# A recurrence and two expert layers: the router's ranks move behind U's products, one list is loaded earlier

## The chip, the cores and the metric

The kernel runs on one core of a Trainium2 chip. The metric is the device time of one execution in microseconds (us), from its first to its last instruction and what lies around them. Engines: PE (TensorE, matmuls), DVE (VectorE), ACT (ScalarE), POOL (GpSimd) and SP (SyncE, which issues DMAs here).

## The reference

Three stages follow one another: a recurrence over 768 steps (4 batches, 8 heads, dimension 40), a mixture of 8 experts with one expert chosen per token, and a second such layer with a bias by modality.

```python
for t in range(S):
    y[:, :, t] = np.einsum('bhd,bhde->bhe', rt, state)
    Sa = np.einsum('bhde,bhe->bhd', state, at)
    state_decay = state * wt[:, :, None, :] - np.einsum('bhd,bhe->bhde', Sa, bt)
    state = state_decay + np.einsum('bhd,bhe->bhde', vt, kt)
...
logits = x @ w_gate
expert_idx = np.argmax(logits, axis=1)
...
for e in range(E):
    mask = expert_idx == e
    ...
    h = np.maximum(xe @ w1[e], 0.0)
    ye = h @ w2[e]
    out[mask] = gate_w[mask, None] * ye
```

Tokens are the 3072 pairs of batch and step, with 320 features each (8 heads of 40); N = 3072, D = 320, E = 8, F = 1024.

## The kernel before

**Attention (some 45 to 500 us).** The 768 steps are cut into 24 chunks of 32 (`cc`, written c0 to c23 here). The instructions stand in the order in which the code issues them (`tc.manual_schedule()`, loop L743 to L849), and each engine works through its own queue in that order. A chunk issues on PE, one after the other: `x_v` (tile `xps`, L524), the transposes of the token rows of chunk cc−2 (`hook1`, `xt`, L1669), `x_z` (`xps`, L526 or L531), the transposed state (`sps`, L572), y's products of the chunk before (`yps`, L610), U's products (`ups`, L542, which ACT copies into `vu`, L546), the first half of y (`yps`, L600), z's products (`zz`, L557, added into the state `zs` by DVE, L563 and L565), `vps` (L582) and `cps` (L591, masked into `csb` by DVE, L594). Between these stand matmuls that prepare chunks ahead: `aps`, `kps`, `aab` (L336, L349, L361; DVE masks `aab` into `ak`, L366). A table `plan` says in which chunks this A-work is done: 13 of the chunks from c3 on (c3, c4, c6, c7, c8 to c16).

On DVE a list of filler work (`fl`, L397 and L403 and others: a triangular solve, transposes and decays of later chunks) is spread between the steps by `fl.run`. Each call issues a share of it; so the order on DVE is fixed when the kernel is built. The same holds for `PADS`, a table of matmuls of no use (`wps`, L883) that keep PE occupied; an entry hangs on a step by name. Two entries hang on `rp`: eleven in c3 and two in c8.

**The router inside the attention.** For the tokens of a finished chunk the loop does the first layer's routing in four steps, spread over three chunks:

- y's product is multiplied by the gate into the token rows `x` (DVE L1662) and stored (POOL's queue, L1663);
- `hook1` (chunk cc−2): transposes `xt`;
- `hook2` (chunk cc−2): the logits `lp` (PE L1677), and `choose` on DVE (`mx`, `dl`, `tb`, `fi`, `oh`, `ent`: L973 to L981) with the exponential on ACT (L975). In the 13 chunks of `plan` it stands right behind U's products, in the others behind `v_t`;
- `hook3` (chunk cc−3): three small matmuls `rp` (PE L990, L991, L992), which count the tokens of each expert up to each token from `oh`, the running counts `ccnt` (POOL L993) and the experts' bases; `tq`, `ps`, `posi` on DVE (L999, L1000, L1002) pick each token's rank; an indirect DMA on POOL's queue (L1011) scatters the token's entry to its place in the list `lst[0]`.

`lp`, `rp` and `aab` use the same PSUM tag "ac" with one buffer (`bufs=1`), so each waits until the one before it has been read.

**Experts (from some 500 us).** Rows are worked in blocks. For a block, `load1` and `load2` bring its weights (SP's queue, L1210 to L1216), `entries` brings its part of the list (`le`, SP's queue, L1250), `gather` fetches the token rows by it (`xg`, POOL's queue, L1257), and `put` stores rows (L1369). In `block(b, prev, nxt)` the work for the block after is issued inside the work for `b`: `entries(nxt)` (unless `begun`), `load1(nxt)`, `gather(nxt)`, and at the end `load2(nxt)`. The first call is `block(b0, a0, b1, begun=True)`; in the next one, `block(b1, b0, bs[1])`, the list of `bs[1]` is loaded.

Of the kernel before, what the change touches and what calls it, by code (L numbers as in the profile page):

```python
# [55 lines left out]
def attention(tc, zones, ident, r, k, v, w, a, b, emit_x, hook0, hook1, hook2, hook3, unsafe, extra, tail):  # L56
    nc = tc.nc
    with ExitStack() as ctx:
        cp = ctx.enter_context(tc.tile_pool(name="a_const", bufs=1))
        wp = ctx.enter_context(tc.tile_pool(name="a_work", bufs=2))  # L60
        ps = Warm(tc, ctx.enter_context(tc.tile_pool(name="a_psum", bufs=1, space=PSUM)), ident)
# [8 lines left out]
        cut = lambda z, at, *shape: view(zones[z], at, *shape)  # L70
# [17 lines left out]
        def guard_load(i):  # L88
            nc.sync.dma_start(out=gtile[i], in_=w.rearrange("b h (z s) d -> (b h z) (s d)", z=4)[:, GN * i : GN * i + GN])
# [73 lines left out]
        def load_a(st, cs=range(4)):  # L163
            st["ar"] = ar = cut("pa", (L + 1) * D, 4, H, D)
            for c in cs:
                t0 = (4 * st["g"] + c) * L
                for bb in range(4):
                    nc.sync.dma_start(out=ar[32 * bb : 32 * bb + 32, c], in_=a[bb, :, t0 : t0 + L, :].rearrange("h t d -> t h d"))
# [489 lines left out]
        def solve_ops(st):  # L658
            ops = solve(st)
            return [(0.19 if 0 < i < len(ops) - 1 else 1.2, f) for i, f in enumerate(ops)]  # L660

        with tc.manual_schedule():
# [80 lines left out]
            for cc in range(NCH):  # L743
                g, c = cc // 4, cc % 4
                nx = Chunk(sts[(cc + 1) // 4], (cc + 1) % 4, rv[cc + 1]) if cc + 1 < NCH else None
                slots = late
                late = [[] for _ in range(8)]
                for ca, how in plan.get(cc, []):
                    sa, ga = sts[ca // 4], ca // 4
                    fs = chunk_a(sa, ca % 4)  # L750
                    if ca % 4 == 3 and ga + 1 < NG:
                        slots[LOADA].append(lambda ga=ga: load_a(sts[ga + 1]))
                    for sl, f in zip(HOW[how], fs):
                        if sl < 0:
                            f()
                        elif sl < 10:
                            slots[sl].append(f)
                        else:
                            late[sl - 10].append(f)
                    if ca % 4 == 3:  # L760
                        def start(sa=sa, ga=ga):
                            if ga == 1:
                                so = hv2.ops()
                                so[0]()
                                fl.add(cc, 2, [(0.14 if i < 60 else 1.8, f) for i, f in enumerate(so[1:])])
                                fl.add(3, 4, [(0.2, f) for f in hv2.rest()])
                            else:
                                so = solve_ops(sa)
                                so[0][1]()
                                fl.add(cc, 4 * ga - 1, so[1:])  # L770
                        (late[{2: 1, 5: 0, 7: 1}[how]] if how in (2, 5, 7) else slots[6]).append(start)

                if cc == 0:
                    nc.gpsimd.memset(kbt[2], 0.0)
                    hv2 = Halves(sts[1])
                if cc == 1:
                    late[0].append(hv2.begin)
                if cc == GUARD:
                    guard_load(0)
                    guard_load(1)  # L780
                    gd = guard_ops(0)
                    gd.append(lambda f=gd.pop(): (f(), guard_load(2)))
                    gd += guard_ops(1) + guard_ops(2)

                def slot(i):
                    if GUARD < cc < VERDICT and i in (1, 2, 4, 5) and gd:
                        gd.pop(0)()
                    for f in todo.get((cc, i), []) + slots[i]:
                        f()
                    for f in extra.get((cc, i), []):  # L790
                        f(ps)
                    if (cc, i) in halves:
                        halves[cc, i]()

                fl.begin(cc)
                ps.at(cc)
                cur.x_v()
                if cc > 2:
                    hook3(cc - 3, ps)
                if cc > 1:  # L800
                    hook1(cc - 2, ps, ident)
                slot(0)
                if cc == 2:
                    hook0(1)
                if cc == VERDICT:
                    verdict()
                cur.x_z()
                cur.s_t(0)
                fl.run(0.2)
                slot(1)  # L810
                if prev:
                    prev.y_c()
                cur.s_t(1)
                fl.run(0.15)
                if nx:
                    nx.r_t()
                if cc + 2 < NCH:
                    rv.append(load_r(cc + 2))
                slot(7)
                cur.u_()  # L820
                fl.run(0.1)
                slot(2)
                if cc > 1 and plan.get(cc):
                    hook2(cc - 2, ps)
                fl.run(0.1)
                cur.y_s()
                fl.run(0.15)
                slot(3)
                fl.run(0.1)
                cur.z_()  # L830
                if cc == 0:
                    spread_ops(sts[1])[3]()
                if nx:
                    cur.z_up(nx.st["qlf"], nx.c)
                slot(4)
                cur.v_t()
                if cc + 2 < NCH:
                    load_v(cc + 2, rv[cc + 2])
                if cc == 0:
                    hook0(0)  # L840
                slot(5)
                if cc > 1 and not plan.get(cc):
                    hook2(cc - 2, ps)
                fl.run(0.07)
                cur.c_()
                slot(6)
                fl.run(0.13)
                fl.drain(cc)
                prev, cur = cur, nx  # L849
# [41 lines left out]
def view(t, at, *shape):  # L891

    n = int(np.prod(shape))
    names = [f"d{i}" for i in range(len(shape))]
    v = t[:, at : at + n]
    return v.rearrange(f"p ({' '.join(names)}) -> p {' '.join(names)}", **dict(zip(names[1:], shape[1:]))) if len(shape) > 1 else v
# [261 lines left out]
class Block:  # L1158
    def __init__(self, lay, tab, j, cut=None, first=False, ready=False, own=None):

        self.lay, self.tab, self.j, self.first, self.ready, self.own = lay, tab, j, first, ready, own
        self.cut, self.i = cut or lay.cut, None


class Rows:
# [23 lines left out]
class Experts:  # L1189
# [56 lines left out]
    def entries(self, b):  # L1246
        nc, c = self.nc, b.cut
        self.place(b)
        r = nc.values_load(b.tab["reg"][0:1, 2, b.j : b.j + 1], engines=[ET.SP], min_val=0, max_val=LST - c.tb)
        d = nc.sync.dma_start(out=b.le, in_=b.lay.lst[ds(r, c.tb)].rearrange("(h p) w -> p h w", p=c.g))  # L1250
        if self.loose and not b.lay.route:
            self.lrows.after(d.ins)
# [125 lines left out]
    def block(self, b, prev, nxt, hook=None, begun=False):  # L1378
# [12 lines left out]
                self.place(x)  # L1391
        if nxt is not None:
            if not begun:
                self.entries(nxt)
                self.load1(nxt)
                put(0, lambda: self.gather(nxt))
        for q in range(0 if b.ready else 4):
# [198 lines left out]
def network(tc, r, k, v, w, a, b, moe_w_gate, moe_w1, moe_w2, moe2_modality_id, moe2_w_gate, moe2_modality_bias, moe2_w1, moe2_w2, out):  # L1596
    nc = tc.nc
    with ExitStack() as ctx:
# [30 lines left out]
        ex = Experts(tc, wt, ident, rt)  # L1629
# [11 lines left out]
        with tc.tile_pool(name="n_x", bufs=1) as xp:  # L1641
# [38 lines left out]
            def hook3(cc, ps):  # L1680
                rps[cc] = rp = ps.tile([P, 1, NE], F32, tag="ac", name="rp", bufs=1)
                rt.rank(rp)
                rt.scatter(rt.rows(rp), ent[:, cc : cc + 1], lst[0])
# [59 lines left out]
        with ExitStack() as ctx2:  # L1743
# [44 lines left out]
            with tc.manual_schedule():  # L1788
                bs = [b1] + [Block(l1, b1.tab, j) for j in range(1, n1)]
                ex.loose = True  # L1790
                ex.load1(b1)
                ex.gather(b1)
                for h in range(CUT0.h):
                    ex.put(a0, h)
                ex.block(b0, a0, b1, begun=True)
                prev = b0
                for b_, nxt in zip(bs, bs[1:]):
                    ex.block(b_, prev, nxt)
                    prev = b_
                t2 = rt.ahead(tp, 1, CUT2, 2, counts(tp, 1))  # L1800
                more = [Block(l2, t2, j, first=j == 0) for j in range(2)]
                ex.block(bs[-1], prev, more[0])
                tabs = []
                ex.block(more[0], bs[-1], more[1], lambda: tabs.append(rt.table(tp, 2, CUT2, counts(tp, 2), t2)))
                ex.run(more[1:] + [Block(l2, tabs[0], j) for j in range(n2)])
# [18 lines left out]
```

## Time and profile before

| | us |
|---|---|
| median of 3 runs | 1011.77 |
| lowest and highest run | 1007.17, 1011.89 |
| profiled execution, its own time | 1014.81 |
| span in its trace (first to last instruction) | 1012.6 |
| PE busy in the span | 896.7 |
| DVE busy | 695.9 |
| ACT busy | 506.5 |
| POOL busy | 308.8 |

The mean granted TensorE clock of the profiled execution is 0.940 of full speed. The shares are means over two very different parts; what a wait in the attention is worth is read from the windows and timelines there. In a timeline a row is a run of like instructions: its start, its duration, the engine, the line, what it writes and reads, and in brackets how long the engine had been idle before it and what ended that.

### The profile page before, as it was taken

The page shows a single profiled execution, that of the slowest core. Times are in us where ns is not written, and L with a number is a line of the kernel's source. Part 1 is how long each engine was busy: PE and PEld are TensorE (multiplying, and loading weights), DVE is VectorE, ACT ScalarE, POOL GpSimd, SP SyncE. Part 2 cuts the span into 40 slices and gives each one's busy share as a digit, 9 for nine tenths or more (in the row PEclk, how much of TensorE's full clock was granted, in tenths as well). Part 3 has the DMA queues.
Part 4 walks back from the last instruction along what each step waited for, and adds up shares of the span by engine and source line. Part 5 has one row for each costly group of instructions (what it writes and reads, how often), then busy time and mean ns, then how long its engine had stood idle before and what let it go on. Part 6 is the DMA issues. An engine that isn't in the chain of part 4 may idle for free. (4 is left out here: it accounts for less than half of the span.)

```text
span 1012.6 us, 38223 instructions
## 1 busy us (share of the span) xinstructions
PE 896.7 (89%) x16089; PEld 828.0 (82%) x16089; DVE 695.9 (69%) x2023; ACT 506.5 (50%) x991; POOL 308.8 (30%) x361
## 2 busy tenths in 40 slices
PE   8748888887878898877979899999999999999995
PEld 8647777676767787766869899999999999999995
DVE  7799999998997966833545354554554866776762
ACT  6625445454535676624414244444544565665662
POOL 6550021221221210122133325453443433323321
PEclk9769989899989999978889899999999999999998
DMA  5545445443432642325017253535343111371110
GB/s 181 138 131 118 75 106 110 113 99 86 97 87 50 165 93 52 55 68 125 11 39 204 83 138 106 147 89 146 109 137 82 27 47 47 90 208 41 43 38 27
DMA packets 152421, 96.41 MB, mean 95 GB/s; under 512 B 127407, under 2 KB 139585, under 8 KB 151850
## 3 DMA queue, kind: packets, MB, share of 16 engines
q1 hardware_dynamic: 138154, 72.53, 28.6%
q0 software_dynamic: 14080, 21.28, 8.2%
q8 instruction: 130, 2.13, 0.9%
q14 instruction: 57, 0.47, 0.2%
HBM read 112.18 MB, written 14.59 MB: 125 GB/s over the span
## 5 line engine op out<-in xcount | busy, mean ns | idle before, releaser
L1301 PE MATMUL hp<-xs,h 128*128 128x256 f32 (+1 forms) x840 | 156.9, 317 | 0.0
L1312 PE MATMUL yp<-h,hh 128*114 128x320 f32 (+1 forms) x464 | 147.0, 317 | 0.3 <-DMA s<-moe_w 0.3
L1313 PE MATMUL yp<-l,hh 128*114 128x320 f32 (+1 forms) x464 | 144.4, 311 | 0.0
L1314 PE MATMUL yp<-h,hl 128*114 128x320 f32 (+1 forms) x464 | 144.2, 311 | 0.0
L1304 DVE SCALAR_TENSOR_TENSOR hl<-hp,hh 128x456 fp32r<-128x456 f32 (+1 forms) x116 | 76.6, 660 | 90.7 <-ACT hh L1303 90.7
L1301 PEld LDWEIGHTS hp<-xs,h 128*128 128x128 f32 x840 | 124.4, 190 | 3.3
L1303 ACT ACTIVATE hh<-hp 128x456 fp32r<-128x456 f32 (+1 forms) x116 | 66.5, 573 | 110.3 <-PE hp L1301 105.9
L1301 PE MATMUL hp<-xs,l 128*128 128x256 f32 (+1 forms) x504 | 102.5, 312 | 0.0
L1222 DVE TENSOR_TENSOR l<-s,h 128x768 fp32r<-128x768 f32 x88 | 80.7, 956 | 11.0 <-ACT h L1221 8.7
L1312 PEld LDWEIGHTS yp<-h,hh 128*114 128x114 f32 (+1 forms) x464 | 85.4, 184 | 0.6 <-ACT hh L1303 0.5
L1313 PEld LDWEIGHTS yp<-l,hh 128*114 128x114 f32 (+1 forms) x464 | 85.5, 184 | 0.2
L1314 PEld LDWEIGHTS yp<-h,hl 128*114 128x114 f32 (+1 forms) x464 | 85.2, 184 | 0.0
L1257 POOL DMA_INDIRECT xg<-x,le x52 | 61.5, 1182 | 70.7 <-issue 50.7
L1301 PEld LDWEIGHTS hp<-xs,l 128*128 128x128 f32 x504 | 80.1, 190 | 3.1
L1228 DVE TENSOR_TENSOR l<-s,h 128x640 fp32r<-128x640 f32 x88 | 72.6, 825 | 3.2 <-ACT h L1227 3.2
L1369 POOL DMA_INDIRECT out<-yo,ti x28 | 34.0, 1215 | 129.4 <-ACT yo L1365 74.7
L1221 ACT CAST h<-s 128x768 fp32r<-128x768 f32 x88 | 70.4, 835 | 0.2
L1227 ACT CAST h<-s 128x640 fp32r<-128x640 f32 x88 | 63.3, 719 | 0.0
L1011 POOL DMA_INDIRECT lst<-l2e,posi x32 | 40.4, 1263 | 59.7 <-DVE posi L1004 52.4
L993 POOL TENSOR_TENSOR ccnt<-ccnt,oh 128x8 bf16<-128x8 bf16 x24 | 6.4, 267 | 168.9 <-PE rp L991 145.7
L1275 DVE TENSOR_TENSOR xs<-ta,xs 128x456 fp32r<-128x456 f32 (+1 forms) x28 | 18.5, 662 | 55.6 <-ACT xs L1274 55.4
L1274 ACT CAST xs<-ta 128x456 fp32r<-128x456 f32 (+1 forms) x28 | 15.8, 564 | 79.3 <-PE ta L1271 79.3
(365 smaller groups left out, 2021.4 us busy)
## 6 DMA issues: line engine op xcount, KB each, us to landing
s<-moe_w SPq DMA_DIRECT2D x22, 1280.0 KB
s<-moe_w SPq DMA_DIRECT2D x22, 1024.0 KB
s<-moe_w SPq DMA_DIRECT2D x44, 256.0 KB
z_w<-w SPq DMA_DIRECT2D x40, 160.0 KB
z_kb<-k SPq DMA_DIRECT2D x24, 160.0 KB
z_kb<-b SPq DMA_DIRECT2D x24, 160.0 KB
z_pa<-a SPq DMA_DIRECT2D x96, 40.0 KB
rt<-r SPq DMA_DIRECT2D x96, 40.0 KB
```

The source lines that it names most:

```text
L1011: d = self.nc.gpsimd.indirect_dma_start(out=dst, out_offset=IndirectOffsetOnAxis(ap=pi[:, i : i + 1], axis=0), in_=ent[:, i], in_offset=No ...
L1221: nc.scalar.copy(wt["h1"][:, :, s], wt["s1"][:, :, s])
L1222: nc.vector.tensor_sub(wt["l1"][:, :, s], wt["s1"][:, :, s], wt["h1"][:, :, s].bitcast(F32))
L1227: nc.scalar.copy(wt["h2"][:, s], wt["s2"][:, s])
L1228: nc.vector.tensor_sub(wt["l2"][:, s], wt["s2"][:, s], wt["h2"][:, s].bitcast(F32))
L1257: d = self.nc.gpsimd.indirect_dma_start(out=b.xg[:, h], out_offset=None, in_=b.lay.src, in_offset=IndirectOffsetOnAxis(ap=b.le[:, h, 0:1]. ...
L1301: nc.tensor.matmul(out=hp[:, i], lhsT=l, rhs=r, start=k == 0, stop=k == len(ops) - 1)
L1303: nc.scalar.activation(hh[:, s], hp, AF.Relu)
L1304: nc.vector.scalar_tensor_tensor(out=hl[:, s], in0=hp, scalar=0.0, in1=hh[:, s].bitcast(F32), op0=ALU.max, op1=ALU.subtract)
L1312: nc.tensor.matmul(out=yp, lhsT=hh[:, k, t], rhs=wt["h2"][:, k], start=k == 0, stop=False)
L1313: nc.tensor.matmul(out=yp, lhsT=hh[:, k, t], rhs=wt["l2"][:, k], start=False, stop=False)
L1314: nc.tensor.matmul(out=yp, lhsT=hl[:, k, t], rhs=wt["h2"][:, k], start=False, stop=k == 7)
```

## The change

`hook3`, with everything that it issues (three matmuls on PE, three operations on DVE, one operation and one indirect DMA on POOL, and the pads that hang on `rp`), moves from behind `x_v` to behind U's products. In the 13 chunks of `plan` it then stands directly ahead of `hook2`. In the experts' part the list of `bs[1]` is loaded before the first `block` call, and a flag `listed` keeps `block` from loading it again.

```diff
                 cur.x_v()
-                if cc > 2:
-                    hook3(cc - 3, ps)
                 if cc > 1:
                     hook1(cc - 2, ps, ident)
...
                 cur.u_()
+                if cc > 2:
+                    hook3(cc - 3, ps)
                 fl.run(0.1)
                 slot(2)
                 if cc > 1 and plan.get(cc):
                     hook2(cc - 2, ps)
...
-        self.cut, self.i = cut or lay.cut, None
+        self.cut, self.i, self.listed = cut or lay.cut, None, False
...
     def entries(self, b):
         nc, c = self.nc, b.cut
         self.place(b)
+        b.listed = True
...
             if not begun:
-                self.entries(nxt)
+                if not nxt.listed:
+                    self.entries(nxt)
                 self.load1(nxt)
...
+                ex.entries(bs[1])
                 ex.block(b0, a0, b1, begun=True)
```

On PE, c9, around U's products (`ups`), before:

```order
L513 MATMUL rps<-ident,rt 80x128 x4
L349 MATMUL kps<-ident,z_wide 128x128 x4
L542 MATMUL ups<-xs,tt 32x40 x32
L1677 MATMUL lp<-wg_123,xT 128x128 x3
L883 MATMUL wps<-ident 128x128 x2
L600 MATMUL yps<-ssb,rb_158 32x40 x32
```

and after (lines behind L1660 are numbered two higher):

```order
L349 MATMUL kps<-ident,z_wide 128x128 x4
L542 MATMUL ups<-xs,tt 32x40 x32
L990 LDWEIGHTS tri
L990 MATMUL rp<-oh_119,tri 128x8
L991 LDWEIGHTS ones
L991 MATMUL rp<-ccnt,ones 128x8
L992 LDWEIGHTS ones
L992 MATMUL rp<-ebr,ones 128x8
L1679 MATMUL lp<-wg_123,xT 128x128 x3
L883 MATMUL wps<-ident 128x128 x2
L600 MATMUL yps<-ssb,rb_158 32x40 x32
```

The six instructions of `rp`, which stood behind `x_v` (L524) of the same chunk, now stand between `ups` and `lp`.

On DVE, c9, before (`pr` and `z_sol` are the solve's filler work, the transpose to `z_wide` too):

```order
L397 TENSOR_TENSOR pr<-z_sol 128x42
L999 TENSOR_TENSOR tq_120<-rp,oh_119 128x8
L1000 TENSOR_REDUCE ps_115<-tq_120 128x1
L1002 CAST posi_121<-ps_115 128x1
L239 STREAM_TRANSPOSE z_wide<-z_kb 128x40x2x16
L397 TENSOR_TENSOR pr<-z_sol 128x45
L403 TENSOR_TENSOR z_sol<-z_sol,pr 128x14x3
L403 TENSOR_TENSOR z_sol<-z_sol,pr 128x15x3
L397 TENSOR_TENSOR pr<-z_sol 128x56 x2
L403 TENSOR_TENSOR z_sol<-z_sol,pr 128x14x4 x2
L397 TENSOR_TENSOR pr<-z_sol 128x65
L1662 TENSOR_TENSOR x<-yps,gt_151 128x320
```

and after, the same stretch from the filler ahead of `x` on:

```order
L397 TENSOR_TENSOR pr<-z_sol 128x65
L1664 TENSOR_TENSOR x<-yps,gt_151 128x320
L397 TENSOR_TENSOR pr<-z_sol 128x70
L403 TENSOR_TENSOR z_sol<-z_sol,pr 128x13x5
L403 TENSOR_TENSOR z_sol<-z_sol,pr 128x14x5
L397 TENSOR_TENSOR pr<-z_sol 128x78 x2
L403 TENSOR_TENSOR z_sol<-z_sol,pr 128x13x6
L999 TENSOR_TENSOR tq_120<-rp,oh_119 128x8
L1000 TENSOR_REDUCE ps_115<-tq_120 128x1
L1002 CAST posi_121<-ps_115 128x1
L403 TENSOR_TENSOR z_sol<-z_sol,pr 128x13x6
L397 TENSOR_TENSOR pr<-z_sol 128x84
```

The three operations `tq`, `ps`, `posi`, which stood ahead of the transpose and of `x`, now stand behind `x`, between two filler operations of L403, a few rows ahead of `mx` (L973), the first reader of `lp`.

On SP's queue, in the experts' part (`s` is the weights' staging buffer: L1212 writes the last of `load1(b1)`, L1216 is `load2(b1)`; `le` is the list of `bs[1]`), before:

```order
L1212 DMA s_9270<-moe_w 64x1024
L1216 ISA
L1216 DMA s_9271<-moe_w 128x8x320
L1249 TENSOR_LOAD small
L1249 ISA x2
L1250 ISA
L1250 DMA le_14600<-lst_61 114x4x4
```

and after:

```order
L1212 DMA s_9270<-moe_w 64x1024
L1250 TENSOR_LOAD small
L1250 ISA x2
L1251 ISA
L1251 DMA le_14600<-lst_61 114x4x4
L1216 ISA
L1216 DMA s_9271<-moe_w 128x8x320
```

The load of the list now stands ahead of that of the weights' second part.

## Rows read from the trace of the kernel before

**Rows 1.** Windows: busy us by engine, early and late stretch.

```profile
core 0: us, PE busy (x) PEld busy (x) DVE busy (x) ACT busy (x) POOL busy (x), PEclk, DMA share, GB/s
150.00:200.00 50.00, 41.81 (x1389) 35.47 (x1388) 48.93 (x158) 24.45 (x56) 10.37 (x13) 0.93 0.50 112
...
450.00:500.00 50.00, 42.23 (x1278) 35.99 (x1276) 19.91 (x55) 23.20 (x52) 9.11 (x12) 0.84 0.34 87
```

**Rows 2.** PE by line, 100:500: busy, mean | idle before, until.

```profile
L990 PE MATMUL rp<-oh,tri 128*128 128x8 bf16 x22 | 3.9, 176 | 12.4 <-DVE oh L980 6.4 <-DVE z_ak L366 4.2 <-DVE ak L366 1.7
```

**Rows 3.** Waits of DVE, 100:500 us: total, times, longest.

```profile
DVE x L1662 <- PE yps L610: 18.8, 10, 4.3
DVE mx L973 <- PE lp L1677: 12.2, 8, 3.0
```

**Rows 4.** Timeline of DVE, c3: start, duration, operation [idle before].

```profile
138.75 0.49 DVE L1662 TENSOR_TENSOR x<-yps,z_gt 128x320 f32<-128x320 f32 x1 [0.55 <-PE yps L610]
```

**Rows 5.** Timeline of DVE, c11.

```profile
295.12 0.49 DVE L1662 TENSOR_TENSOR x<-yps,gt 128x320 f32<-128x320 f32 x1 [1.61 <-PE yps L610]
```

**Rows 6.** Timeline of PE, beginning of c3.

```profile
129.41 0.18 PE L990 MATMUL rp<-oh,tri 128*128 128x8 bf16 x1 [3.17 <-DVE oh L980]
...
129.65 0.61 PE L1669 MATMUL xt<-ident,x 128*128 128x128 f32 x3
```

**Rows 7.** Timeline of all engines, c13, where lp follows tq.

```profile
331.23 0.16 DVE L999 TENSOR_TENSOR tq<-rp,oh 128x8 f32<-128x8 f32 x1
...
331.45 0.38 PE L1677 MATMUL lp<-wg,xT 128*128 128x128 f32 x1 [0.34 <-DVE tq L999]
```

**Rows 8.** Timeline of PE, c9, from U's products to z's.

```profile
256.81 1.33 PE L542 MATMUL ups<-xs,tt 32*32 32x40 f32 x64
258.06 1.13 PE L1677 MATMUL lp<-wg,xT 128*128 128x128 f32 x6
...
260.97 0.80 PE L600 MATMUL yps<-ssb,rb 128*32 128x40 f32 x64 [1.13 <-DVE x L1662]
...
262.73 1.44 PE L557 MATMUL zz<-vu,kb 128*40 128x80 f32 x32
```

**Rows 9.** Timeline of DVE, c9.

```profile
261.54 1.58 DVE L403 TENSOR_TENSOR z_sol<-z_sol,pr 128x78 f32<-128x78 f32 x2
...
263.52 0.15 DVE L973 TENSOR_REDUCE mx<-lp 128x1 f32<-128x8 f32 x1
...
266.99 0.82 DVE L563 TENSOR_TENSOR zs<-zz,zs 128x640 f32<-128x640 f32 x1
```

**Rows 10.** Timeline of all engines, a late chunk's rp and tq.

```profile
451.41 0.18 PE L990 MATMUL rp<-oh,tri 128*128 128x8 bf16 x1
...
451.76 0.17 DVE L999 TENSOR_TENSOR tq<-rp,oh 128x8 f32<-128x8 f32 x1 [0.38 <-PE rp L992]
```

**Rows 11.** Timeline of SP's queue: weights' second part, then the list.

```profile
533.29 0.39 SPq L1216 DMA_DIRECT2D s<-moe_w  x1
534.84 0.33 SPq L1250 DMA_DIRECT2D le<-lst  x1
```

**Rows 12.** Timeline of ACT: first cast of those weights.

```profile
551.05 0.72 ACT L1227 CAST h<-s 128x640 fp32r<-128x640 f32 x1
```

**Rows 13.** Timeline of POOL: first gather of the block.

```profile
559.25 1.21 POOL L1257 DMA_INDIRECT xg<-x,le  x1 [8.12 <-issue]
```

**Rows 14.** Windows at the beginning of c6.

```profile
190.00:192.00 2.00, 0.14 (x2) 0.13 (x2) 1.79 (x9) 0.21 (x1) 1.67 (x2) 0.86 0.44 73
192.00:197.00 5.00, 5.00 (x142) 4.13 (x141) 4.93 (x12) 1.37 (x4) 0.50 (x2) 0.50 0.60 159
```

**Rows 15.** Timeline of PE at the lower clock: lp and z's products.

```profile
446.79 1.94 PE L1677 MATMUL lp<-wg,xT 128*128 128x128 f32 x6
...
463.63 2.37 PE L557 MATMUL zz<-vu,kb 128*40 128x80 f32 x32
```

**Rows 16.** Timeline of PE: the gathered rows are waited for.

```profile
571.93 0.45 PE L1271 MATMUL ta<-ident,xg 114*128 114x114 f32 x1 [3.85 <-DMA xg<-x,le]
```

## The prediction, made before the changed kernel was run

> **What bounds the kernel now.** I read the windows first. In a window of the early chunks DVE is busy 48.93 us of 50 and PE 41.81; in a window of the last chunks DVE is at 19.91 and PE at 42.23 of 50, at a granted clock of 0.84 [rows 1]. So the attention part has two regimes. Up to about chunk 13 (c13; c8 and c12 are partly exceptions) DVE is the bound, and a wait of PE costs nothing until DVE runs out of work. Later the chain from PE to ACT to DVE and back is the bound, and PE work on it counts in full. Then I read what the moved `rank` matmuls wait for: PE sits 12.4 us before their first matmul, until `oh` or `ak` come from DVE [rows 2]. That looks like a prize, but the view of waits on DVE decides: what DVE itself loses to y's products (`x`) is 18.8 us in 10 waits, and to the logits (`lp`) 12.2 us in 8 [rows 3]. Of the waits for `x`, only two stand in a DVE-bound chunk in which PE had waited before rp: 0.55 us in c3 [rows 4] and 1.61 us in c11 [rows 5].
>
> **What goes.** Between the start of rp and the first transpose behind it lie 129.65 − 129.41 = 0.24 us of PE [rows 6], and in front of rp there is the wait. Both leave the chunk's beginning. In c3 (wait 3.17 us) and c11 DVE gets back no more than its own gap, 0.55 and 1.61; I count 1.75 for c11, because its later products also gain the 0.24. In the late chunks c17 to c22 rp stands on PE's path at the beginning, and its new place behind U's products lies under ACT's copies of U, for which `zz` waits anyway: 6 x 0.24 = 1.44. In c23 a wait of 0.57 goes too: 0.81. Gains: 0.55 + 1.75 + 1.44 + 0.81 = 4.55 us.
>
> **What comes.** In the 13 chunks that still plan A-work, the logits' matmuls follow rp directly. rp and lp share one PSUM buffer (tag "ac"), so lp can't start before `tq` on DVE has read rp. In the kernel before this wait shows once, in c13: lp sits 0.34 us until tq, and starts 0.06 us behind tq's end [rows 7]. Behind lp, on PE's queue, stand y's, z's, v's and c's products; DVE waits for all of them. Two prices follow, by what DVE is doing.
>
> Where DVE is the bound, tq waits for its turn. In c9 its new turn is behind the first of the two L403 at 261.54, which end together at 263.12, the second taking some 0.15: so tq starts at about 262.95 and ends at 263.1, and lp starts at 263.2 instead of 258.06, 5.1 us later [rows 8, 9]. Behind it PE has the same products as before up to zz's end, which came at 262.73 + 1.44 = 264.17, that is 6.11 us behind lp's start, with a wait of 1.13 for `x` among them that is over by then. So zz ends at 263.2 + 4.98 = 268.2, where `zs` of the kernel before started at 266.99. DVE has the same work up to there in both kernels (three rank operations are merely moved), so DVE loses 1.2 us; of the 5.1 us, 3.9 are swallowed by slack. The same reading in c6, c11 and c13 (lp later by 3.5, 5.2 and 4.1 us, the slack of `mx`, `zs` and `csb` taken one by one) gives 0.8, 0.5 and 0.5. In c3, c4, c7 and c10 the slack covers all. Sum 3.0.
>
> Where DVE waits for PE (c8, c12, c14, c15, c16), tq follows rp at once. Where DVE stood ready in the kernel before, rp started at 451.41 and its tq at 451.76, 0.35 later, and lasted 0.17 [rows 10]; with the 0.06 of the way back lp is 0.58 us later, less the 0.24 that left the beginning: 5 x 0.34 = 1.7. Bounds: 5 x 0 if DVE's other waits take it all, 5 x 0.58 = 2.9 if the beginning gives nothing back.
>
> Edits at nothing. POOL's `ccnt` and the scatter now stand behind x's store; POOL is busy 10.37 of 50 us in the early window [rows 1], and the lists are first read after the attention. On DVE three small operations are moved, none added. The eleven and two warming matmuls that hang on rp in c3 and c8 go with it into time in which PE waits (c3) or some tenths (c8, inside the bound of 2.9). The second edit puts the load of `le` ahead of `load2(b1)` on SP's queue: from 533.29 and 534.84 [rows 11] to the reverse order, load2 about 1.5 us later. Its first reader is ACT's cast at 551.05 [rows 12], over 15 us later. The gather that reads `le` comes at 559.25 [rows 13] either way, since it follows the rows that the puts before it store. Zero.
>
> Without the clock: 3.0 + 1.7 − 4.55 = +0.15 us.
>
> **The clock.** The granted clock is the term that decides the sign. In c6 PE had 0.14 us of work in the two microseconds before rp, and from 192 to 197 the clock is 0.50, that is 1.2 GHz [rows 14]. Seven of the eight waits of 2.4 us or more between 129 and 464 us have such a stretch right behind them. The Trainium skill, "TensorE: Matmul & The Clock Gate", section "What's actually happening", says that "the default state is throttled, and activity releases the throttle"; the rows of c6 agree. The rule speaks against this change: by it alone all four new waits would be followed by the half clock, the time of the first rival below. The change makes four new waits of 3.5 to 5.2 us, in c6, c9, c11 and c13, and each lies directly ahead of matmuls whose slack is by then used up. At the half clock lp takes 1.94 instead of 1.13, zz 2.37 instead of 1.44 [rows 8, 15]: 0.81 + 0.93 = 1.74 us for each such chunk. c6 and c11 already have a half-clock stretch, which may only move. For c9 and c13 I take even odds: 2 x 1.74 / 2 = +1.74. Bounds: nothing, or 4 x 1.74 = 6.96.
>
> Sum: 0.15 + 1.74 = +1.9 us. On the profiled run (span 1012.6, its own time 1014.81) that is 1016.7; that run stands 3.04 us above the median of the runs, 1011.77, so I state the forecast against the median: **1013.7 us**. About 0.5% (5 us) is what a measurement of this kernel can tell from no change; the three runs of before differ by 4.7 us among themselves.
>
> **Rivals.**
> *The clock falls in all four chunks* (slower). Mechanism: PE stands behind lp's wait for tq, the clock drops to 1.2 GHz, and lp, zz and what follows come late for DVE, which has no slack left. It decides from two full stretches on. For it: c6's rows, and seven waits of eight. Against it: DVE had filler work in c6 that hid a half-clock stretch completely. Price 0.15 + 6.96 = +7.1: 1018.9. Chance 0.27.
> *The waits at the chunk's beginning were on the path* (faster). PE then runs ahead, and DVE's waits for `x` and `zs` shrink in more chunks than c3 and c11. For it: 12.4 us of PE waiting, the four longest 3.17, 2.68, 1.69 and 1.51, together 9.05; against it: DVE is busy 48.93 of 50 us there, with no room to run ahead. Price −9.05 + 3.0 = −6.05, without the clock: 1005.7. Chance 0.12.
> *The gather at 559.25 was held by `le`*, and the 3.85 us that PE waits for its rows go [rows 16]: 1.9 − 3.85 = −1.95: 1009.8. `le` was issued 24 us earlier, so 0.04.
> *The rank is off the path in both places*, and lp's wait is hidden: 0, 1011.8. Chance 0.07. That the instructions don't move as the edit says is excluded by their order.
>
> **How the numbers follow.** Forecast (−1 to +5) 0.50, clock in full 0.27, faster 0.12, gather 0.04, nothing 0.07. Predicted is the likeliest, 1013.7. The range reaches from 1007.5 (runs of an unchanged kernel come as low as 1007.2, and half of the faster case) to 1019.5 (clock in full, with the upper bound of 2.9). Faster by over 0.5%: 0.12 + 0.02 = 0.14. Slower by over 0.5%: 0.27 and the upper edge of the forecast, 0.30. Within: 0.56.
>
> **What would show it.** In the profile after: rp directly ahead of lp; a new wait of PE `lp` for DVE `tq` in 13 chunks, 3.5 us and more in c6, c9, c11, c13; the wait before rp for `oh` and `ak` gone; DVE's gaps before `x` in c3 and c11 closed; the late chunks 0.24 shorter each; new stretches at 0.50 behind lp in c9 and c13, or none; the gather at the same distance from the puts. The forecast is wrong if PE's lead at the beginning shortens chunks in which DVE shows no gap for `x`, or if the half clock comes in all four chunks.

## The result, and the profile after

The changed kernel took 1023.16 us in the median of 4 runs (1015.14 to 1026.52), beside 1010.26 us for the kernel before (4 runs); the ratio is 1.0114, 95% interval [1.0069, 1.0159]. The forecast was 1013.7 us with a range up to 1019.5: it is missed on the slow side. Run again later in 12 runs beside others of before, the same kernel gave 1.0029 [0.9986, 1.0072] (e22 below), and with the first edit alone 1.0112 (e1). So the rank's new place costs time, by the mean of these three 0.85% or 8.6 us. The ratios leave out runs more than 1.5% above the fastest run of their kernel, in e22 three of 12 (1028.5 to 1031.5 us), and the means of all its runs would give 1.0060. A ratio from one set of runs is no better than about half a per cent, whatever its interval says: two kernels that were run twice came out 0.0085 and 0.0056 apart. What follows rests on groups of kernels and on what recurs in several traces.

The profiled execution took 1020.81 us. Waits of PE, 100 to 505 us, changed kernel (total, times, longest):

```profile
PE lp L1679 <- DVE tq L999: 18.8, 13, 5.1
...
PE rp L990 <- DVE ak L366: 0.2, 1, 0.2
```

Waits of DVE, 100 to 500 us, changed kernel:

```profile
DVE tq L999 <- PE rp L992: 21.8, 12, 3.5
DVE x L1664 <- PE yps L610: 21.7, 11, 4.7
DVE zs L563 <- PE zz L557: 13.9, 5, 8.0
DVE mx L973 <- PE lp L1679: 7.9, 10, 1.2
```

To set beside the third line, from the kernel before:

```profile
DVE zs L563 <- PE zz L557: 20.4, 7, 10.0
```

The waits of [rows 2] in front of rp are gone but for 0.2 us; in their place stands PE's wait at `lp` for `tq`, in 13 chunks. The longest four are those of c6, c9, c11 and c13: 5.09, 3.37, 3.43 and 3.25 us. Beside [rows 3], DVE's waits for `x` grew from 18.8 to 21.7 us, those for `mx` fell from 12.2 to 7.9 and those for `zs` from 20.4 to 13.9, and a line of 21.8 us has come that the prediction never priced: DVE standing at `tq` until rp is done (0.9 us before).

c9 on PE, changed kernel (to be read against [rows 8]):

```profile
262.31 0.18 PE L990 MATMUL rp<-oh,tri 128*128 128x8 bf16 x1
...
266.00 1.95 PE L1679 MATMUL lp<-wg,xT 128*128 128x128 f32 x6 [3.37 <-DVE tq L999]
267.87 1.22 PE L883 MATMUL wps<-ident 128*128 128x128 f32 x4
269.02 1.29 PE L600 MATMUL yps<-ssb,rb 128*32 128x40 f32 x64
...
272.15 1.04 PE L557 MATMUL zz<-vu,kb 128*40 128x80 f32 x22
```

c9 on DVE, changed kernel (against [rows 9]):

```profile
265.79 0.15 DVE L999 TENSOR_TENSOR tq<-rp,oh 128x8 f32<-128x8 f32 x1
...
267.98 0.17 DVE L973 TENSOR_REDUCE mx<-lp 128x1 f32<-128x8 f32 x1 [1.03 <-PE lp L1679]
...
273.62 0.82 DVE L563 TENSOR_TENSOR zs<-zz,zs 128x640 f32<-128x640 f32 x1 [1.98 <-PE zz L557]
```

rp is done by 262.6, but tq's turn on DVE comes at 265.79, and lp starts 0.06 us behind tq's end, as in c13 of the kernel before [rows 7]. lp then lasts 1.95 instead of 1.13 us and the pads 1.22 instead of 0.71: the granted clock is 0.50 there, called the half clock below. `mx` and `zs`, which waited for nothing in [rows 9], now wait 1.03 and 1.98 us. Windows of the changed kernel: c6's wait and what follows, the same for c9, and what follows the waits of c11 and c13:

```profile
core 0: us, PE busy (x) PEld busy (x) DVE busy (x) ACT busy (x) POOL busy (x), PEclk, DMA share, GB/s
200.20:205.40 5.20, 0.11 (x2) 0.02 (x2) 5.17 (x21) 1.64 (x4) 1.47 (x2) 0.87 0.47 74
205.40:211.00 5.60, 5.60 (x80) 4.63 (x80) 5.09 (x25) 0.82 (x3) 1.25 (x2) 0.51 0.10 29
262.60:266.00 3.40, 0.03 (x2) 0.01 (x1) 3.37 (x18) 1.74 (x5) 0.71 (x1) 0.92 0.43 68
266.00:272.00 6.00, 6.00 (x82) 5.05 (x82) 4.37 (x26) 0.79 (x3) 2.23 (x4) 0.50 0.79 162
...
308.00:312.00 4.00, 3.95 (x74) 3.27 (x74) 2.65 (x20) 0.21 (x1) 1.93 (x2) 0.50 0.12 18
...
343.50:348.00 4.50, 4.45 (x90) 3.58 (x92) 3.54 (x20) 0.75 (x2) 2.28 (x4) 0.62 0.92 376
```

PE works 0.11 and 0.03 us in the two waits, and behind all four the granted clock is 0.50 to 0.62 of full speed, that is the 1.2 GHz level for most of each stretch. In the chunks' lengths (from a chunk's first `x_v` matmul to the next one's) c6, c9, c11 and c13 together last 90.2 us in this trace and 82.5 in that of before. A chunk's beginning is a point on PE, so part of such a difference can be time that the next chunk gets back; c4 to c16 as a whole last 245.6 us here and 237.8 before.

c3 is another story. PE in c3, changed kernel:

```profile
139.33 1.13 PE L542 MATMUL ups<-xs,tt 32*32 32x40 f32 x64
140.39 2.72 PE L883 MATMUL wps<-ident 128*128 128x128 f32 x22
142.95 0.17 PE L990 MATMUL rp<-oh,tri 128*128 128x8 bf16 x1
```

and DVE there:

```profile
139.59 0.21 DVE L490 TENSOR_TENSOR z_sol<-z_sol,pr 128x56 f32<-128x56 f32 x1
143.28 0.17 DVE L999 TENSOR_TENSOR tq<-rp,oh 128x8 f32<-128x8 f32 x1 [3.49 <-PE rp L992]
```

The eleven pads (22 matmul passes, 2.72 us) went with rp to behind U's products and stand in front of it, while DVE, which is the bound here, waits 3.49 us for rp. DVE's wait for `x` in c3 [rows 4] and that in c11 [rows 5] are gone, as the prediction said; in c3 the wait for rp has taken its place.

### The profile page after: what moved, and what is told of

It reads as the page before. It is cut to its first block, busy times and chain, and to the rows that moved or that the text cites. A ratio compares the mean times of both kernels' runs of the same rounds, so it can differ in the third digit from the quotient of the medians.

```text
span 1019.1 us, 38211 instructions
## 1 busy us (share of the span) xinstructions
PE 893.1 (88%) x16089; PEld 823.4 (81%) x16089; DVE 693.9 (68%) x2023; ACT 506.0 (50%) x991; POOL 299.6 (29%) x361
## 5 line engine op out<-in xcount | busy, mean ns | idle before, releaser
L1665 POOL DMA_DIRECT2D x<-x x24 | 18.5, 771 | 244.5 <-DVE z_sol L403 112.5
L1315 PEld LDWEIGHTS yp<-h,hl 128*114 128x114 f32 (+1 forms) x464 | 85.1, 183 | 0.0
L1228 DVE TENSOR_TENSOR l<-s,h 128x640 fp32r<-128x640 f32 x88 | 72.5, 825 | 2.0 <-ACT h L1227 2.0
```

The lines of the kernel that those rows point to most:

```text
L1228: nc.vector.tensor_sub(wt["l2"][:, s], wt["s2"][:, s], wt["h2"][:, s].bitcast(F32))
L1315: nc.tensor.matmul(out=yp, lhsT=hl[:, k, t], rhs=wt["h2"][:, k], start=False, stop=k == 7)
```

## The experiments

All times are ratios to the kernel before, run on the same chip in the same rounds. "Four chunks" is the summed length of c6, c9, c11 and c13 in the experiment's own trace.

| kernel | rank behind U in | rp's buffer | ratio, 95% interval | four chunks, us |
|---|---|---|---|---|
| before | none | shared | 1 | 82.5 |
| e2 list only | none | shared | 0.9988 [0.9951, 1.0025] | 80.8 |
| e10 buffer only | none | own | 0.9985 [0.9950, 1.0021] | 82.0 |
| e8 late | c17 to c23 | shared | 0.9957 [0.9917, 0.9997] | 80.4 |
| e9 middle | c8, c12, c14 to c16 | shared | 1.0003 [0.9957, 1.0049] | 80.9 |
| the changed kernel | all | shared | 1.0114 [1.0069, 1.0159] | 90.2 |
| e22 the same again | all | shared | 1.0029 [0.9986, 1.0072] | 89.0 |
| e1 rank only | all | shared | 1.0112 [1.0072, 1.0153] | 93.0 |
| e3 pads stay | all | shared | 1.0043 [1.0011, 1.0075] | 90.1 |
| e7 four | c6, c9, c11, c13 | shared | 1.0039 [1.0003, 1.0074] | 90.6 |
| e4 pads before lp | all | shared | 1.0035 [1.0003, 1.0066] | 83.6 |
| e6 e3 and e4 | all | shared | 1.0083 [1.0043, 1.0122] | 85.7 |
| e17 e7 and e4 | the four | shared | 1.0074 [1.0041, 1.0107] | 83.1 |
| e18 e3, wide pads | all | shared | 1.0060 [1.0024, 1.0096] | 91.0 |
| e19 e7, wide pads | the four | shared | 1.0023 [0.9983, 1.0063] | 81.7 |
| e5 own buffer, pads stay | all | own | 0.9943 [0.9905, 0.9981] | 82.6 |
| e20 the same again | all | own | 0.9999 [0.9966, 1.0032] | 76.4 |
| e14 rows later | all | own | 0.9963 [0.9928, 0.9998] | 76.7 |
| e21 own buffer, pads moved | all | own | 0.9966 [0.9927, 1.0004] | 76.8 |
| e16 four, own buffer | the four | own | 0.9984 [0.9947, 1.0021] | 76.1 |

**The two edits apart: e1 and e2.** e1 leaves `ex.entries(bs[1])` where it was, e2 keeps the rank where it was.

> The rank behind U's products as in the changed kernel, the list loaded where the kernel before loads it. Theory: the whole loss comes from the rank's place, so this is 1.1 to 1.3% slower than before, with the chunks c3, c6, c9, c12 and c13 longer by 1.4 to 3.8 us each as in the changed kernel. Rival, the earlier list costs or gives: the ratio differs from the changed kernel's 1.011 by more than 0.3%.

> The list of the second full block loaded early, the rank where the kernel before has it. Theory: no change, within 0.2% of before; the gather that reads the list still starts about 9 us behind the last put. Rival, the gather was held by the list: the 3.85 us that PE waits for its rows go, 0.4% faster. Rival, the load stands in the way of the weights on the queue: slower by 0.2% or more.

e1 has the whole loss, e2 none that shows. SP's queue and POOL's in e2:

```profile
536.68 0.32 SPq L1251 DMA_DIRECT2D le<-lst  x1
537.36 0.41 SPq L1216 DMA_DIRECT2D s<-moe_w  x1
```

```profile
552.28 1.13 POOL L1370 DMA_INDIRECT x<-yo,small  x1 [0.30 <-issue]
561.01 1.21 POOL L1258 DMA_INDIRECT xg<-x,le  x1 [7.61 <-issue]
```

The list now goes ahead of the weights, and the gather still starts 8.7 us behind the last put's issue (in the kernel before 559.25 against 550.01, 9.2). The list was issued 24.3 us before the gather here and 24.4 us before it there, so it came no nearer to holding it or to letting it go; that the list did not hold it is argued from this distance, and from PE's wait for the gathered rows (3.85 us before [rows 16]), which is 0.7 us in e2 but 4.6 in the changed kernel with the same early list. The second edit is worth nothing that these runs can show.

**The pads that went along: e3.**

```diff
-(3, 'rp', 0): 11, ... (8, 'rp', 0): 2
+(3, 'xt', 0): 11, ... (8, 'xt', 0): 2
```

> The changed kernel, but the eleven warming matmuls of c3 and the two of c8 stay at the chunk's beginning (ahead of the transposes xt). Theory: c3 is 1.8 to 2.5 us shorter than in the changed kernel, since DVE's wait of 3.49 us for rp there was the pads in front of rp; in all 0.2% less than the changed kernel, about 1.009 to 1.010 of before. Rival, DVE would wait in c3 for another reason: c3 stays at 30.9 us.

DVE in c3 of e3:

```profile
138.94 0.21 DVE L490 TENSOR_TENSOR z_sol<-z_sol,pr 128x56 f32<-128x56 f32 x1
139.77 0.17 DVE L999 TENSOR_TENSOR tq<-rp,oh 128x8 f32<-128x8 f32 x1 [0.62 <-PE rp L992]
```

DVE's wait at tq falls from 3.49 to 0.62 us, and c3 lasts 28.2 us instead of 30.9. This recurs: with the rank moved, c3 lasts 30.9 to 32.3 us in the five traces in which the pads went along and 27.5 to 29.7 in the six in which they stayed. In the total it can't be told: e3 (1.0043, where 1.009 to 1.010 was expected) is 0.7% under the changed kernel's first ratio but 0.14% above its second, and e21 against its like with the pads left behind (e5, e14, e20: mean 0.9968) shows nothing.

**Filling the waits: e4, e6, e17, then e18 and e19.** e4 puts pads between rp and lp, e6 does so in e3, e17 in e7 (the rank moved in four chunks alone, `if cc > 2 and cc in (6, 9, 11, 13)`):

```diff
+(6, 'lp', 0): 14, (9, 'lp', 0): 9, (11, 'lp', 0): 9, (13, 'lp', 0): 9
```

e18 and e19 do the same to e3 and e7 with 13 matmuls of 128x512 (4, 3, 3 and 3) in place of 41.

> The changed kernel with warming matmuls between rp and lp: 14 in c6, 9 in each of c9, c11 and c13, sized to the time in which PE waits there for tq. They fill the wait and lengthen none. Theory of the clock: lp and z's products then run at full clock, the gaps of DVE before mx and zs in c9 (1.03 and 1.98 us) shrink, and the four chunks together are 4 to 7 us shorter, ratio about 1.006. Rival, the waits themselves and not the clock cost: no chunk gets shorter, ratio 1.011 as in the changed kernel.

> As e3, with the pads between rp and lp of e4. Theory: the two parts of the loss are apart and both are given back: 1.0112 less 0.7% less 0.7%, ratio 0.997 to 1.000. Rival, e3 and e4 gave back the same thing (a lead or lag that shifts all that follows): ratio 1.003 to 1.005, as each alone.

> The rank behind U's products only in c6, c9, c11 and c13; in all other chunks, pads included, as the kernel before. Theory: these four carry the loss of the long waits and the half clock: 5 to 8 us, ratio 1.005 to 1.008. Rival, the loss is spread over all chunks by DVE's waits for rp: ratio below 1.003.

> As e7 (moved only in c6, c9, c11, c13, shared buffer), with the pads of e4 between rp's place and lp in these chunks. Theory of the clock: the four chunks fall from 90.6 us to 84 to 86, as in e4 and e6, DVE's gaps before zs in c9 (1.80) vanish, and the ratio is 0.3% to 0.6% under e7's 1.0039. Rival: what the pads give back in the four chunks is lost again in others (as e6 against e3 suggests), ratio as e7 or above.

> As e3, with few wide pads (128x512) ahead of lp: 4 in c6, 3 each in c9, c11, c13, some 1 us each at full clock; 13 matmuls in place of the 41 of e6. Theory of the clock: the half clock behind lp costs in all; without the added instructions of e6 the ratio falls 0.3% to 0.6% under e3's 1.0043. Rival: the clock is paid in the four chunks but given back later; the four chunks fall to 84 to 86 us and the ratio stays at 1.003 to 1.006.

> As e7, with the same wide pads in its four chunks. Theory of the clock: 0.3% to 0.6% under e7's 1.0039. Rival: the four chunks fall from 90.6 us to 83 to 86, the ratio stays at 1.003 to 1.006; e17's 1.0074 was then not the pads' instructions alone.

Windows of e4 behind the four waits:

```profile
205.80:211.00 5.20, 5.20 (x121) 4.58 (x120) 4.96 (x23) 1.96 (x4) 1.98 (x2) 1.00 0.18 40
...
264.20:269.00 4.80, 4.79 (x114) 4.20 (x114) 4.34 (x25) 1.84 (x4) 2.26 (x4) 1.00 0.78 181
...
305.60:309.00 3.40, 3.40 (x100) 2.94 (x102) 2.89 (x19) 1.13 (x3) 1.95 (x2) 1.00 0.09 15
...
338.60:343.00 4.40, 4.38 (x126) 3.75 (x130) 3.94 (x22) 1.37 (x3) 2.27 (x4) 1.00 0.81 230
```

e7, with the rank moved in the four chunks alone, has their full length (90.6 us) and a ratio of 1.0039, some half of the loss, between its theory and its rival.

With PE occupied, the clock stays at 1.00 in e4 where it was 0.50 to 0.62, and the four chunks together last 83.6 us instead of 90.2. e6, e17 and e19 come near that (85.7, 83.1, 81.7); in the 5 us behind lp their clock is 1.00 too, but for c6 and c9 of e6 (0.67, 0.68) and c11 of e17 (0.66). In e18 the wide pads did not hold the clock in c9 (lp runs from 262.81):

```profile
263.00:266.00 3.00, 3.00 (x50) 2.39 (x53) 2.23 (x12) 0.21 (x1) 2.05 (x3) 0.56 0.79 148
266.00:270.00 4.00, 4.00 (x72) 3.58 (x66) 2.46 (x14) 1.75 (x3) 0.00 (x0) 0.50 0.76 177
```

and its four chunks stay at 91.0, though in the other three the clock was 1.00. So in four kernels of five these chunks are 5 to 9 us shorter where the half clock is mostly gone. DVE says the same: its idle time in the four chunks (their length less its busy time) is 3.5 to 5.6 us in the five traces with the rank at its old place there, 7.8 to 13.2 in the changed kernel, e22, e1, e3 and e7, 3.0 to 6.6 in e4, e6, e17 and e19, and 9.6 in e18.

But the total does not follow. e4 lies between the changed kernel's two ratios, e6 is above e3 by 0.4% (0.997 to 1.000 was expected), e17 above e7 by 0.35%, e18 above e3 by 0.17%, e19 below e7 by 0.16%; the five kernels with filled waits have a mean of 1.0055, the five of the same kind without (changed kernel, e22, e1, e3, e7) 1.0067. The traces show where it went in the three kernels with 41 pads: c8, c12 and c14 to c16 together last 86.8, 88.8 and 92.8 us in e4, e6 and e17 and 81.1 to 85.1 in those five, and DVE is idle there for 36.4 to 38.2 us, in the 17 other traces for 25.1 to 34.6 (their lengths there reach 86.9 in e2 and 88.6 in e16). So c4 to c16 as a whole last 246.4, 247.2 and 249.3 us with the waits filled and 244.8 to 247.6 without. I tried fewer instructions (e18, e19) because more of them might be what cost there. e19, with 13 pads, lasts 82.3 us in those middle chunks and 241.6 from c4 to c16, as with the rank at its old place (237.8 to 242.2); e18 lasts 246.3. One trace and a ratio of 1.0023 don't show that the number of pads is the reason: why the middle chunks grew stays open.

**Taking the wait away: e5, e20, e14, e16, with e10 as control.** rp moves to a tag with three buffers, so that lp needs no tq:

```diff
-rp = ps.tile([P, 1, NE], F32, tag="ac", name="rp", bufs=1)
+rp = ps.tile([P, 1, NE], F32, tag="tp", name="rp", bufs=3)
```

> As e3 (pads at the chunk's beginning), and rp takes a slot of the tag tp (three buffers) in place of ac, so that lp no longer waits until tq has read rp. Theory: the long waits of PE for tq in c6, c9, c11 and c13 are gone or far shorter, with them the half-clock stretches behind lp; those four chunks are 5 to 8 us shorter than in e3 together, ratio about 0.998. Rival, DVE's own waits for rp at tq cost: they stay (17.8 us in e3), and the ratio stays near e3's 1.004.

> The same kernel as e5 once more, beside other runs of before. Theory: rp in its own buffer, the rank behind U's products and the pads left at the beginning beat the kernel before, ratio 0.992 to 0.998. Rival: e5's 0.9943 was the luck of its runs, ratio 0.998 to 1.002.

> The kernel before, with rp in a slot of the tag tp in place of ac; nothing moved. Theory: at the chunk's beginning the shared buffer cost almost nothing (lp waits once for tq, 0.34 us, and aab 0.6 us), so the ratio is 0.998 to 1.000: the gain of e5 (0.9943) then needs the move and the buffer together. Rival: the buffer alone gives it, since rp no longer waits for oh and ak behind aab; ratio 0.994 to 0.996.

> As e7 (moved only in c6, c9, c11, c13), with rp in tp. Theory: the long waits of PE for tq in these chunks (16.5 us in e7) vanish; the four chunks fall from 90.6 us to 81 to 83; ratio 0.5% to 0.9% under e7's 1.0039. Rival: DVE's operations of the rank in their new place cost as much by themselves, the four chunks stay above 88 us.

c9 in e20, on PE:

```profile
258.38 0.19 PE L990 MATMUL rp<-oh,tri 128*128 128x8 bf16 x1
...
258.64 1.31 PE L1679 MATMUL lp<-wg,xT 128*128 128x128 f32 x6
...
260.53 0.84 PE L600 MATMUL yps<-ssb,rb 128*32 128x40 f32 x64
```

and on DVE:

```profile
259.45 0.15 DVE L999 TENSOR_TENSOR tq<-rp,oh 128x8 f32<-128x8 f32 x1
...
260.53 0.16 DVE L973 TENSOR_REDUCE mx<-lp 128x1 f32<-128x8 f32 x1
...
264.78 0.81 DVE L563 TENSOR_TENSOR zs<-zz,zs 128x640 f32<-128x640 f32 x1
```

lp follows rp after 0.26 us and no longer waits for tq at 259.45; `mx` and `zs` wait for nothing. The four chunks last 76.1 to 76.8 us in e14, e16, e20 and e21 (82.6 in e5, where c6 alone has a DVE wait of 4.1 us for a DMA, at most 0.3 in the other four). The times agree: the five kernels with the rank moved in these chunks and rp's own buffer have ratios of 0.9943 to 0.9999, mean 0.9971; the ten with the shared buffer 1.0023 to 1.0114, mean 1.0061. No kernel of one group reaches the other. The pair that differs in the buffer alone, e7 and e16, is 0.55% apart. The difference of the groups, 0.9%, is some 9 us; the four chunks show 8 to 14 (90.6, the mean of the five unfilled traces, against 76 to 83), but c4, c5, c7 and c10 are longer by some 6 with rp's own buffer (77.0 to 80.2 us against 70.7 to 73.5), and c4 to c16 as a whole show 4.7 (mean 246.4 against 241.6). The buffer alone, with the rank at its old place, gives nothing (e10, 0.9985).

**DVE's wait at tq: e14.** It issues tq, ps, posi and the scatter behind the first filler share after U's products.

> As e5, and tq, ps, posi and the scatter are issued one filler share later, behind the first fl.run after U's products, so that DVE stands less at tq for rp (16.4 us in 12 waits in e5). Theory: that wait only takes the place of those for lp and zz, which stand right behind it in the late chunks; so no change against e5, ratio 0.993 to 0.997. Rival: the wait for rp is on the path, some 3 to 6 us less, ratio 0.990 or below.

It gives 0.9963, between e5 and e20: no change. But it took away only a part of the wait, which is 16.4 us in e5, 20.1 in e20 and still 13.4 in e14. What settles more are the waits of DVE in e20:

```profile
DVE x L1664 <- PE yps L610: 24.9, 10, 8.0
DVE tq L999 <- PE rp L992: 20.1, 12, 3.4
```

DVE waits 20.1 us at tq there, nearly as much as the 21.8 of the changed kernel, in a kernel that is not slower than before. So the largest new line in the view of waits is not what makes the changed kernel slow. That DVE stands at tq for what it would else stand for at `mx` or `zs` fits their lines in the changed kernel, which fell by 4.3 and 6.5 us; what the wait at tq costs by itself was not measured.

**The middle and the late chunks: e9 and e8.**

> The rank behind U's products only in c8, c12, c14, c15 and c16, shared buffer, else as before. Prediction on record: 0.34 us lost in each, 1.7 in all, ratio 1.0 to 1.003. Rival: rp, tq and the way back count in full and with the pads' move to c8 more, 3 to 5 us, ratio 1.003 to 1.005.

> The rank behind U's products only in c17 to c23, elsewhere as the kernel before. Prediction on record: 0.24 us gained in each, some 2.2 us in all, ratio 0.998. Rival: DVE's waits for rp at tq (0.8 to 2.6 us in each of these chunks in the changed kernel) are on the path, ratio 1.002 or more.

e9 agrees with the 1.7 us on record as far as a ratio can tell. e8's ratio lies on the side of the gain forecast, but its trace doesn't show one: c17 to c22 last 97.3 us in e8, 94.5 in before and 91.6 in e2, which have the rank at its old place. Its size, and whether it is one, stays open.

**The last pair: e21 and e22.** e21 is e5 with the pads moved along, e22 the changed kernel again.

> As e5, but the eleven pads of c3 and the two of c8 go with rp, as in the changed kernel. Theory: the pads in front of rp cost some 2.7 us in c3 (30.9 to 31.9 us against 28.2) whatever buffer rp has: c3 is 30 to 32 us, ratio 0.2% to 0.4% above the mean of e5, e14 and e20 (0.997), so about 1.000. Rival: the pads cost only together with the shared buffer, ratio as e5, e14 and e20.

> The changed kernel itself once more, in the same rounds as e21. Theory: 1.1% slower than before as in its first runs and in e1, ratio 1.008 to 1.013. Rival: the first runs were unlucky by some tenths as e5 and e20 were apart by 0.5%, ratio 1.004 to 1.007, as e3 and e7.

Both came out lower than theory had them. c3 of e21 is 32.3 us, near the 30 to 32 expected; the total doesn't show it. e22 gives a quarter of the first ratio's loss. The pair itself, 0.9966 against 1.0029, is again the buffer's price, 0.6%.

A version that beats both kernels: the rank behind U's products with rp in its own buffer and the pads left behind was run twice and was under before the first time and level with it the second; 0.9943 and 0.9999 together don't make it clearly faster than before. It is faster than the changed kernel (1.0114, 1.0029).

## Why the prediction was wrong, point by point

- **The mechanism was right, its size was not.** lp behind rp in one buffer, 13 waits for tq, the long ones in c6, c9, c11, c13: as forecast (lp later by 3.5, 5.1, 5.2 and 4.1 us on record, waits of 5.09, 3.37, 3.43 and 3.25 measured). e16 against e7 and e5, e14, e20 against e3 show that this wait is the cause of the loss. The Trainium skill's "Perfetto Trace Analysis", section "Matmuls", asks for independent matmul groups to rotate through different PSUM banks; the 0.9% between the two groups of kernels agrees with it.
- **The step that failed is the even odds on the clock for c9 and c13 alone.** In the trace the clock fell to 1.2 GHz behind all four waits, as in the first rival. For these chunks the forecast had 3.0 for the wait, 1.74 for the clock and 1.75 of gain in c11, net 3.0 us; that rival 3.0 + 6.96 − 1.75 = 8.2. Measured: 90.6 less 81.3 us (means of five traces each, the changed kernel, e22, e1, e3 and e7 against before, e2, e8, e9 and e10), 9.3 us. c9 shows it on DVE: the forecast had DVE lose 1.2 us, with the half clock 2.9, and it stands 1.03 us at `mx` and 1.98 at `zs`, 3.0 in all. DVE's idle time in the four chunks grew by 6.6 us (mean 10.9 in the first five traces, 4.2 in the second) and is 4.6 in the mean of e4, e6, e17 and e19: by this estimate from single traces 0.3 us come with the wait alone, where the forecast had 3.0 − 1.75, and 6.3 with the half clock, where it had 1.74 and 6.96 as the bound. My own count, seven waits of eight with the half clock behind them, stood against my even odds, and I argued that two stretches would merely move; with the rank at the old place c6's stretch lay in time that DVE's filler hid, in the new place it lies behind lp, where DVE waits.
- **That step is not the whole miss.** c4, c5, c7 and c10 got back 2.4 of the 9.3 us (72.5 against 74.8), and c4 to c16 as a whole grew by 6.2 (246.4 against 240.2), where the forecast's terms for this stretch, 3.0 + 1.74 − 1.75 + 1.7, give 4.7. The total grew by 8.6 instead of 1.9. Of these 6.7 us, 1.5 are seen in that stretch, 2.8 are gains that did not show (c3's 0.55 and the late 2.25), and the rest is within what the ratios leave open. The first rival's time, 1018.9, that is +0.7%, is the nearest to the mean of 0.85%, but since filled waits did not lower the total, how much of the total is the clock and how much the wait itself is not shown.
- **c3: a step that was wrong outright.** "Into time in which PE waits" was read from the chunk's beginning, where PE did wait 3.17 us [rows 6]. Behind U's products PE did not wait, and the pads delayed rp by 2.7 us with DVE waiting for it. The gain of 0.55 did not come; c3 of the changed kernel is no shorter than that of before (30.9 against 29.2 us). With the pads left behind it came, and larger, some 3 us. The 0.55 itself was a low row: in the eight other traces with c3's rank at the old place (e2, e7 to e10, e16, e17, e19) DVE waits 1.8 to 3.3 us for `x` there.
- **The gain in c11** of 1.75 us is not to be seen in the changed kernel's chunk (20.9 us against 21.1): DVE's wait for `x` is gone, and lp's wait takes its place. With rp's own buffer c11 lasts 16.4 to 19.2 us.
- **The faster rival** looks half right in the four chunks, which with rp's own buffer are 4 to 5 us under the old place (not in e5). But c4, c5, c7 and c10 are as much longer (77.0 to 80.2 us against 71.8 to 77.2), and c4 to c16 last 238.3 to 243.4 us against 237.8 to 242.2. In the total 0.15 to 0.3% is left (0.9971 against e2, e10 and 1).
- **The late gain of 2.25 us:** open (e8). **The middle chunks, 1.7 us:** not contradicted (e9). **The list, zero:** right as far as e2 can tell (0.9988); nothing in it or in the changed kernel speaks for the rival on the gather.
- **What was not priced:** DVE's own wait for rp, 21.8 us, the largest change in any view. It does not explain the loss (20.1 us in e20), but the prediction never looked at it.
- **The range** left the slow side too short. The before runs known then spread by 4.7 us; in later sets they spread from 1000.65 to 1025.72. The mean loss of 0.85% would be 1020.4, just outside the range; by e22 alone the time would have been inside it.

## What to carry to other kernels

When a step moves next to another that uses the same single buffer, the reader between them becomes a wait of the engine, and its turn on the other engine's queue, not its own length, sets the price: look up where the reader stands in that queue, or give the step a buffer of its own. Warming matmuls that hang on a step by name move with it; in a new place they are work in front of somebody. A large new line in a view of waits is not yet a loss: look for it in a kernel that did not slow down. And a chunk that got longer or shorter is not yet a price: add up its neighbours too.

## What the runs showed of the hardware that was not expected

- The half clock is local and easy to see (0.50 to 0.62 behind waits with 0.03 to 0.12 us of PE work in them, 1.00 where e4's pads filled them, four chunks 5 to 9 us shorter in four kernels of five), yet over five pairs of kernels it left no trace in the total (means 1.0055 and 1.0067). In the three kernels with 41 pads c8, c12 and c14 to c16 took the gain back.
- Stretches in which PE waits for nothing that the profile shows ("issue") of 1 to 5 us wander between chunks from one execution to the next: c20 lasts 14.5 us in one trace of the shared-buffer kernels (e1) and 19.9 in another (the changed kernel), with the same instructions. One trace of a chunk is not enough to price some tenths of a microsecond. From c23 on, where the kernels hardly differ, the 20 traces last 519.0 to 533.5 us, so totals differ by more than the change does for reasons that lie outside it.
